# Another order of all queues for a routed attention with a gated dense block behind it

## The chip, the cores and the metric

The kernel runs on one core of one Trainium2 chip. A core has TensorE (PE, the matrix engine, whose weight loads are listed apart as PEld), VectorE (DVE), ScalarE (ACT), GpSimd (POOL), and SyncE (SP), which here only issues transfers. Each of them works through its own queue in the order in which the program was written; between the queues only semaphores order the work. The metric is the device time of one execution in microseconds; less is better.

## The reference

The inputs are q, k and v of 4 batches, 8 heads, 768 tokens and 64 values, and 16 centroids for each head. Every token of q and k is given to the centroid of its head that it is most alike, and a token of q attends only to the tokens of k with the same centroid:

```
mask   = q_assign[:, :, :, None] == k_assign[:, :, None, :]
scores = where(mask, q @ k.T / sqrt(D), -1e9)
attn   = softmax(scores);   a = attn @ v
x   = a, heads side by side          # 3072 x 512
h   = x @ w_in                       # 3072 x 1024
u   = h * softmax(h)
out = ((u - mean(u)) / sqrt(var(u) + 1e-6) * g_ln) @ w_out
```

## The kernel before

**The work.** A head's queries and keys are laid out with 64 rows of values and 16 or 32 rows of marks (which centroid), so that one product gives the score with the mask in it. The heads are taken in pairs, four pairs a batch, sixteen in all. For a pair, q and k are loaded by SyncE (`ld`), turned so that tokens lie along the free side (in batch 0 by TensorE, `tp`, and copied out of PSUM by `xa` and `xt`; later by VectorE, `xt`), cast to bf16 (`ca`), multiplied with the centroids (`cl` on TensorE), and the best centroid is found on VectorE (`tb`, `mx`, `oh`, `ot`) and placed as marks behind the cast values (`pl`; `bl` clears rows). v is loaded (`lv`) and cast (`cv`). Names carry batch, pair, q or k and half, so `ca0.2.1.1` is batch 0, pair 2, k, second half.

**The attention.** The scores are made in 144 regions of 1024 columns. `S` fills a region in two halves on TensorE (L641), `E` takes the exponential on ScalarE (L651), `V` multiplies with v on TensorE (six matmuls of 65 columns, L663), and `N` normalises on VectorE and frees the one bank that the V of a group write. Two PSUM regions are used in turn for S, so S of a region waits for the E two before. Batch 0 is regions 0 to 35.

**The dense block.** It runs on 24 tiles of 128 tokens, beside the attention of the next batch. x is turned by a transposing transfer (`tx`), `h` is the first product (four parts of two matmuls, L772), `hm` finds the maximum on VectorE and frees the bank, `ex` is the exponential on ScalarE, `u` the product with h, `tu` a transposing transfer, `bn`, `ag`, `as`, `al` the statistics, `y` the second product (L844) into one bank, `sc` scales it out of the bank, on ScalarE (L856) or VectorE (L858), and `ou` stores. The weights are loaded by `li` and `lo`, w_in is cast (`wi`), and w_out is centred by its column sums (`me`, `mf`, `ce`). The last tile is split finer and turned by TensorE (`ptx`, `ptu`).

**The order.** Nothing is planned when the kernel is built: each step is added under its name with the engine it may run on, and one list, `ORDER`, gives the sequence in which all 1568 steps are written. Each engine's queue is what falls to it from that list. A table, `AWAY`, names the steps that run on another engine than the one given in the code; `on(name, engine)` looks it up. The loop that writes the program is

```
for name in ORDER:
    o = self.ops[name]
    assert done.issuperset(o["first"]) and name not in done, name
    ...
    o["fn"]()
```

and it demands only that what a step needs has been written before it. A step that stands early in its engine's queue and waits holds everything behind it on that engine, transfers on SyncE included.

Of the kernel before, what the change touches and what calls it, by code (L numbers as in the profile page):

```python
# [45 lines left out]
E0 tp0.2.1.1 xt0.2.1 S1.0 tp0.3.0.0 S1.1 S2.0 S2.1 tp0.3.0.1 tb0.1 mx0.1 oh0.1 xa0.3.0 E1 E2 cl0.2  # L46
xt0.3.0 S3.0 S3.1 V0.0 V0.1 V1.0 S4.0 S4.1 V1.1 tp0.3.1.0 tb0.2 E3 S5.0 S5.1 E4 E5 ot0.1 N0 mx0.2
gt tp0.3.1.1 S6.0 S6.1 V2.0 V2.1 S7.0 S7.1 V3.0 V3.1 xa0.3.1 gk xt0.3.1 cl0.3 E6 E7 cv0.1.0
pl0.1.1.1 ca0.1.0.1 ca0.3.0.0 pl0.1.1.0 ca0.3.0.1 z2 ca0.1.1.1 oh0.2 pl0.1.0.0 pl0.1.0.1 gw S8.0
S8.1 S9.0 S9.1 me0 me1 ot0.2 tb0.3 pl0.2.1.0 N1 pl0.2.0.0 mx0.3 mk oh0.3 ca0.2.0.0 ca0.2.1.0  # L50
ca0.3.1.0 ca0.2.1.1 pl0.2.1.1 pl0.2.0.1 E8 E9 ca0.2.0.1 S10.0 S10.1 S11.0 S11.1 V4.0 V4.1 V5.0
V5.1 E10 S12.0 S12.1 cv0.2.1 E11 E12 mf N2 ot0.3 pl0.3.0.0 ld1.0.0.0 li0 ld1.0.0.1 ld1.0.0.2
ld1.0.0 ld1.0.1.0 lv0.3 ld1.0.1.1 ld1.0.1.2 ld1.0.1 cv0.1.1 ca0.3.1.1 pl0.3.1.0 pl0.3.0.1 cv0.2.0
cv0.3.0 cv0.3.1 wi0 S13.0 S13.1 V6.0 V6.1 S14.0 S14.1 V7.0 V7.1 pl0.3.1.1 N3 km ce0 E13 E14 S15.0
S15.1 S16.0 S16.1 E15 E16 V8.0 V8.1 S17.0 S17.1 E17 V9.0 V9.1 S18.0 S18.1 E18 S19.0 S19.1 N4 ce5
V10.0 V10.1 V11.0 V11.1 S20.0 S20.1 E19 S21.0 S21.1 E20 E21 li1 li3 N5 V12.0 V12.1 ptx0 S22.0
# [1298 lines left out]
```

## Time and profile before

| | |
|---|---|
| median of 3 runs | 222.33 us (221.85 to 222.96) |
| the profiled execution | 222.33 us |
| its span | 220.5 us |
| instructions | 6292 |
| granted TensorE clock | 1.00 in every stretch |

The profile's page gives first the busy time of each engine and its share of the span, then the span in forty slices, the chain of work that ended last, and groups of instructions by line. A row of the chain or of the order of time has the start in us, the length in us, the engine and line. A row of a group has the count, the busy time, the mean length in ns, and the idle time just before, with what ended it. A busy TensorE is not a TensorE at its peak, since its instructions overlap and may wait inside its pipe.

### The profile page before, as it was taken

The numbers are of one execution on the slowest core, as the hardware profiler recorded it, in microseconds if no ns is written. First come the engines' busy times: TensorE is split into PE (matmuls) and PEld (weight loads), VectorE is DVE, ScalarE is ACT, GpSimd is POOL, SyncE is SP. The second block draws the span as 40 slices with busy tenths as digits, with TensorE's granted clock in tenths as the row PEclk, the third lists the DMA queues.
The fourth block names the chain that finished last, engine by engine and source line by source line (L and its number), as shares of the span: only waits on it lengthen the run. The fifth ranks groups of instructions, "written<-read, shape, count | busy, mean of one in ns | idle before, by whom it ended". The sixth has DMA issues, their size and how long they took to land.

```text
span 220.5 us, 6292 instructions
## 1 busy us (share of the span) xinstructions
PE 211.4 (96%) x2401; PEld 148.9 (68%) x2431; DVE 185.7 (84%) x430; ACT 192.8 (87%) x245; POOL 158.8 (72%) x198
## 2 busy tenths in 40 slices
PE   7899999999999999999999999999999999999984
PEld 4567577677678776777677677666777767655442
DVE  3699979968999999896799999994888856989982
ACT  3799999999999998999999989999999888685362
POOL 3686969897898999549939997879889054456610
PEclk9999999999999999999999999999999999999999
DMA  5998999999999993999999981939584229777522
GB/s 199 394 402 259 189 175 300 126 154 259 164 154 169 190 188 62 174 248 210 153 225 162 180 184 38 171 92 209 151 173 90 72 64 168 154 120 170 163 94 100
DMA packets 120911, 38.33 MB, mean 174 GB/s; under 512 B 109993, under 2 KB 116401, under 8 KB 120881
## 3 DMA queue, kind: packets, MB, share of 16 engines
q1 hardware_dynamic: 120448, 37.40, 81.7%
q10 hardware_dynamic: 432, 0.52, 0.7%
q8 instruction: 19, 0.31, 0.6%
q14 instruction: 12, 0.09, 0.2%
HBM read 23.11 MB, written 6.29 MB: 133 GB/s over the span
## 4 chain that ended last, share of the span: by engine, by line
PE 72%; DVE 10%; DMA 6%; POOL 5%; issue 3%; ACT 2%; SPq 1%; DVEq 0%; ACTq 0%; POOLq 0%
PE sb L641 22%; PE hb L772 16%; PE mb L844 15%; PE ob L663 12%; DMA w_st<-in_moe_w_in_dram 4%; PE hb L470 3%; DMA raw<-in_q_dram 2%; DVE w_st L782 2%; PE hb L396 2%; DVE xt L421 2%; DVE bs L816 2%; POOL kbig L441 1%; PE mb L470 1%; POOL w_in_sb L580 1%; POOL v L556 1%
## 5 line engine op out<-in xcount | busy, mean ns | idle before, releaser
L651 ACT ACTIVATE e<-sb 128x1024 bf16<-128x1024 f32 x144 | 139.9, 1024 | 8.9 <-PE sb L641 8.1
L641 PE MATMUL sb<-qbig,kbig 80*128 80x256 bf16 (+3 forms) x648 | 83.8, 261 | 1.3 <-ACT e L651 1.0
L641 PEld LDWEIGHTS <-kbig 80*128 80x128 bf16 (+1 forms) x648 | 62.9, 119 | 25.4 <-issue 8.6
L805 POOL TENSOR_TENSOR u<-e_sb,w_st 128x1024 bf16<-128x1024 bf16 x21 | 45.1, 2145 | 20.0 <-ACT e_sb L798 13.3
L663 PEld LDWEIGHTS <-e 128*128 128x128 bf16 x1152 | 48.6, 97 | 10.4 <-DVE x L686 0.6
L663 PE MATMUL ob<-v,e 128*128 128x65 bf16 x1140 | 51.4, 193 | 0.2
L772 PE MATMUL hb<-w_in_sb,xT 128*128 128x512 bf16 x173 | 50.6, 379 | 0.9 <-POOL v L1323 0.3
L844 PE MATMUL mb<-w_out_c,uT 128*128 128x512 bf16 x165 | 45.5, 379 | 1.2 <-DVE y L858 0.4
L816 DVE BATCH_NORM_STATS2 bs<-u 128x6 f32<-128x512 bf16 x48 | 31.6, 680 | 1.1 <-POOL u L805 1.1
L798 ACT ACTIVATE e_sb<-w_st,nmax 128x1024 bf16<-128x1024 f32 (+1 forms) x25 | 27.8, 1113 | 3.2 <-DVE w_st L782 1.8
L439 POOL CAST qbig<-xt 64x768 bf16<-64x768 f32 (+1 forms) x31 | 25.7, 830 | 6.5 <-PE ob L663 2.7
L441 POOL TENSOR_SCALAR kbig<-xt 64x768 bf16<-64x768 f32 (+1 forms) x32 | 27.6, 865 | 2.4 <-DVE xt L409 0.8
L840 POOL TENSOR_TENSOR alpha<-var,halves 128x1 f32<-128x1 f32 x24 | 15.3, 638 | 12.6 <-DVE var L823 8.0
L421 DVE STREAM_TRANSPOSE xt<-raw 128x768 f32<-128x768 f32 x24 | 22.5, 959 | 0.1
L844 PEld LDWEIGHTS <-uT 128*128 128x128 bf16 x176 | 15.2, 97 | 10.2 <-issue 0.8
L772 PEld LDWEIGHTS <-xT 128*128 128x128 bf16 x192 | 15.8, 98 | 8.8 <-issue 0.6
L686 DVE TENSOR_TENSOR x<-ob,den 128x256 bf16<-128x256 f32 (+2 forms) x40 | 19.0, 474 | 1.4
L782 DVE TENSOR_SCALAR_CACHE_REDUCE w_st<-hb 128x512 f32<-128x512 f32 x24 | 16.3, 680 | 3.8 <-PE hb L772 3.7
L782 DVE TENSOR_SCALAR_CACHE_REDUCE w_st<-hb,nmax 128x512 f32<-128x512 f32 x24 | 17.8, 740 | 1.9 <-PE hb L772 1.5
L856 ACT ACTIVATE y<-mb,alpha 128x512 f32<-128x512 f32 x15 | 10.3, 685 | 6.5 <-POOL alpha L840 3.6
L675 DVE RECIPROCAL den<-ob 128x4 f32<-128x4 f32 (+2 forms) x40 | 7.1, 178 | 10.4 <-PE ob L663 10.1
L556 POOL CAST v<-vf 128x384 bf16<-128x384 f32 x22 | 10.9, 504 | 3.3 <-DMA vf<-in_v_dram 2.6
(109 smaller groups left out, 202.6 us busy)
## 6 DMA issues: line engine op xcount, KB each, us to landing
vf<-in_v_dram SPq DMA_DIRECT2D x16, 384.0 KB, 5.3
out_dram<-y SPq DMA_DIRECT2D x23, 256.0 KB, 2.5
raw<-in_k_dram SPq DMA_DIRECT2D x26, 192.0 KB, 4.6
raw<-in_q_dram SPq DMA_DIRECT2D x24, 192.0 KB, 5.1
...
raw<-in_q_dram SPq DMA_DIRECT2D x3, 384.0 KB, 6.6
raw<-in_k_dram SPq DMA_DIRECT2D x3, 384.0 KB, 7.6
```

The costliest lines, as they stand in the source:

```text
L421: nc.vector.transpose(xts[b, p, i][:], raw_of(b, p, i))
L439: (nc.vector if e == "DVE" else nc.gpsimd).tensor_copy(dst, src)
L441: (nc.vector if e == "DVE" else nc.gpsimd).tensor_scalar(dst, src, scalar1=inv_C, scalar2=1.0, op0=Alu.mult, op1=Alu.mult)
L641: nc.tensor.matmul(reg[:, c:c + wd], kb[u, pp, side_of(h), keys], qb[u, pp, side_of(h), su * P:su * P + wd])
L651: nc.scalar.activation(es[r][:, :w], src, Act.Exp, scale=exp_scale, bias=-exp_scale)
L663: nc.tensor.matmul(ops_of(group_of[n])[:, s, :VW], es[r][:, c0:c0 + P], v1[index[b, pair_of(h)] % R][:, side_of(h), kt, :VW], start=(kt == ...
L772: nc.tensor.matmul(hb[f2][:], xTs[f][:, dc, :], w_in_sb[:, dc, f2 * BANK:(f2 + 1) * BANK], start=(dc == 0), stop=(dc == n_dc - 1))
L782: nc.vector.tensor_scalar(ff[f, "h"][:, f2 * BANK:(f2 + 1) * BANK], hb[f2][:], scalar1=-1.0, scalar2=nmax[:, f2 - 1:f2] if f2 else 3.0e38, ...
L798: nc.scalar.activation(ff[f, "e"][:, cols(f, f2)], ff[f, "h"][:, cols(f, f2)], Act.Exp, bias=ff[f, "nmax"][:, n_ff2 - 1:], scale=-1.0, acc ...
L805: (nc.vector if e == "DVE" else nc.gpsimd).tensor_tensor(ff[f, "u"][:, cols(f, f2)], ff[f, "e"][:, cols(f, f2)], ff[f, "h"][:, cols(f, f2) ...
L816: nc.vector.bn_stats(ff[f, "bs"][:, f2, :], ff[f, "u"][:, f2 * BANK:(f2 + 1) * BANK])
L844: nc.tensor.matmul(y_of(f, x), ff[f, "uT"][:, fc, :], w_out_c[:, fc, parts_of(f, x)], start=(fc == 0), stop=(fc == n_fc - 1))
```

## The change

`AWAY` and `ORDER` are replaced. The set of the 1568 steps, their dependencies, the tiles and the buffers are the same; every queue has another order, and 77 steps run on another engine:

- from ScalarE to VectorE: the scalings sc6, sc7, sc8, sc11, sc17, sc22, the copy xa0.3.0 and the placing pl0.1.1.1; back: sc16 and xt0.2.1
- from ScalarE to GpSimd: four casts of q or k, eight of v, three placings; back: six casts of q or k, four of v, two placings
- from VectorE to GpSimd: nine `as`, eight placings, ce4 and ce5, bl1.2 and bl3.0, u20; back: five `as`, nine placings, bl2.0 and bl3.2, u0 and u15

On SyncE the first load of v stands behind three loads of tokens instead of one, the first load of w_in (`li0`) comes ahead of three of w_out's, and `lv0.3` ahead of batch 1's loads. The diff, cut to the table of engines, the start, the first steps of batch 1 and the end:

```diff
-    ca0.0.1.1.0 ca0.2.0.1 ca1.0.0.1 ca3.1.1.0 ca3.2.0.1 cv0.0.1 cv0.1.0 cv0.2.1 cv1.2.0
-    cv1.3.1 cv2.0.1 cv2.1.0 cv3.0.0 cv3.0.1 cv3.3.0 pl0.0.0.1 pl0.0.1.0 pl0.1.1.1 pl2.2.1.0
-    xa0.0.0 xa0.1.0 xa0.1.1 xa0.2.0 xa0.2.1 xa0.3.0 xt0.1.0 xt0.1.1 xt0.2.0 xt0.3.0
+    ca0.0.1.0.1 ca0.2.1.1 ca0.3.1.1 ca2.2.1.0 ca3.2.0.1 ca3.3.0.1 cv0.1.0 cv3.0.1 cv3.1.1
+    cv3.2.0 cv3.2.1 cv3.3.1 pl0.0.0.0 pl0.0.1.1 xa0.0.0 xa0.1.0 xa0.1.1 xa0.2.0 xa0.2.1
+    xt0.1.0 xt0.1.1 xt0.2.0 xt0.2.1 xt0.3.0
...
-    as0 as11 as14 as15 as17 as18 as19 as2 as22 as23 as4 as5 as9 bl1.2 bl3.0 ce0 ce2 ce4 km mk
...
-    pl1.2.0.0 pl2.0.0.0 pl2.0.0.1 pl2.0.1.1 pl2.2.0.0 pl3.0.0.1 pl3.2.0.1 pl3.2.1.0 sc0 sc1
-    sc12 sc13 sc14 sc16 sc4 sc9
+    as1 as12 as13 as14 as17 as18 as2 as20 as8 bl2.0 bl3.2 ce0 ce2 km mk pl0.0.1.0.0 pl0.1.1.1
+    pl0.2.1.0 pl0.2.1.1 pl0.3.0.1 pl0.3.1.0 pl0.3.1.1 pl1.0.0.0 pl1.0.1.0 pl1.0.1.1 pl1.2.0.0
+    pl1.2.1.0 pl2.0.0.0 pl2.0.1.0 pl2.0.1.1 pl2.2.0.0 pl3.0.1.1 pl3.2.0.0 pl3.2.1.0 sc0 sc1
+    sc11 sc12 sc13 sc14 sc17 sc22 sc4 sc6 sc7 sc8 sc9
...
-lc ld0.0.0.0 ld0.0.1.0 ld0.0.0 ld0.0.1 ld0.1.0 ld0.1.1 lv0.0 ld0.2.0 ld0.2.1 ld0.3.0 lo3 lv0.1
-ld0.3.1 lg lv0.2 lo1 lo2 lo0 cx z5 cy cz wu tp0.0.0.0 tp0.0.0.1 tp0.0.1.0 tp0.0.1.1 cp xa0.0.0
-xt0.0.0 xa0.0.1 xt0.0.1 tp0.1.0.0 xa0.1.0 cb cl0.0 tb0.0 mx0.0 oh0.0 ot0.0 ca0.0.0.0.0 z3
-ca0.0.1.0.0 ca0.0.0.0.1 cc ca0.0.0.1.1 ca0.0.0.1.0 pl0.0.1.1 pl0.0.0.0 ca0.0.1.0.1 ca0.0.1.1.1
-ca0.0.1.1.0 tp0.1.0.1 tp0.1.1.0 xt0.1.0 xa0.1.1 cl0.0.1 tp0.1.1.1 cv0.0.1 xt0.1.1 pl0.0.0.1
-tp0.2.0.0 tp0.2.0.1 tb0.0.1 mx0.0.1 oh0.0.1 ot0.0.1 pl0.0.1.0.1 pl0.0.1.0.0 pl0.0.1.1.1 cl0.1 sg
-pl0.0.1.1.0 z1 ca0.1.1.0 cv0.0.0 ca0.1.0.0 xa0.2.0 pl0.0.1.0 tp0.2.1.0 xt0.2.0 xa0.2.1 S0.0 S0.1
+lc ld0.0.0.0 ld0.0.1.0 ld0.0.0 ld0.0.1 ld0.1.0 ld0.1.1 lg ld0.2.0 ld0.2.1 ld0.3.0 lv0.0 lo0
+ld0.3.1 li0 lo2 lo3 lo1 lv0.1 lv0.2 cx cy cz wu tp0.0.0.0 tp0.0.0.1 tp0.0.1.0 tp0.0.1.1 xa0.0.0
+xt0.0.0 ca0.0.0.0.1 xa0.0.1 cp tp0.1.0.0 cb cl0.0 tb0.0 mx0.0 oh0.0 ot0.0 xt0.0.1 ca0.0.1.0.1
+xa0.1.0 tp0.1.0.1 xt0.1.0 tp0.1.1.0 xa0.1.1 tp0.1.1.1 xt0.1.1 cl0.0.1 tp0.2.0.0 tp0.2.0.1 tb0.0.1
+mx0.0.1 oh0.0.1 ot0.0.1 pl0.0.1.0.0 cl0.1 tb0.1 pl0.0.1.0.1 ca0.0.0.0.0 ca0.0.0.1.0 ca0.0.1.0.0
+ca0.0.0.1.1 cc ca0.0.1.1.0 ca0.1.0.0 pl0.0.1.0 pl0.0.0.1 sg ca0.0.1.1.1 pl0.0.1.1.1 pl0.0.1.1.0
+pl0.0.1.1 pl0.0.0.0 xa0.2.0 tp0.2.1.0 xt0.2.0 xa0.2.1 S0.0 S0.1 E0 tp0.2.1.1 tp0.3.0.0 S1.0 S1.1
...
-S28.1 E28 V16.0 V16.1 V17.0 S29.0 S29.1 h0.1.0 V17.1 S30.0 S30.1 E29 E30 oh1.0 hm0.0 N8 ot1.0 ce2
-pl1.0.1.0 pl1.0.0.1 pl1.0.1.1 bl1.0 ce3 lv1.0 tx2 lv1.1 lv1.2 ld2.0.0.0 ld2.0.0.1 ld2.0.0.2 h0.1.1
-S31.0 S31.1 V18.0 V18.1 V19.0 S32.0 S32.1 V19.1 h1.0.0 N9 hm0.1 pl1.0.0.0 xt1.2.0 E31 S33.0 S33.1
+S28.1 E27 E28 V16.0 V16.1 V17.0 S29.0 S29.1 V17.1 h0.0.1 S30.0 S30.1 oh1.0 N8 h0.1.0 E29 E30 S31.0
+S31.1 E31 V18.0 V18.1 V19.0 S32.0 S32.1 V19.1 h0.1.1 ot1.0 pl1.0.1.1 hm0.0 pl1.0.1.0 N9 pl1.0.0.0
+xt1.2.0 hm0.1 S33.0 S33.1 h1.0.0 ca1.0.0.1 ca1.0.0.0 pl1.0.0.1 ca1.0.1.0 ca1.1.0.1 z4 ca1.0.1.1
...
-y20.0 y20.1 y20.2 y20.3 sc20 hm23.0 bn22.0 h23.1.1 ptu22.0 ptu22.1 bn22.1 hm23.1 tu22.1 tu22.0
-ex23.0 ex23.1 ou19 y21.0 y21.1 y21.2 y21.3 ou20 u23.0 u23.1 ag22 as23 ptu23.0 ptu23.1 tu23.1
-bn23.0 bn23.1 ag23 al21 sc21 ou21 tu23.0 y22.0 y22.1 y22.2 y22.3 y23.1.0 y23.1.1 y23.1.2 y23.1.3
-y23.0.0 y23.0.1 y23.0.2 y23.0.3 al22 sc22 al23 sc23.0 sc23.1 ou23.1 ou22 ou23.0
+y20.2 y20.3 sc20 h23.1.1 hm23.0 hm23.1 ptu22.0 ptu22.1 bn22.0 tu22.1 ex23.0 ex23.1 tu22.0 y21.0
+y21.1 y21.2 y21.3 ou19 ou20 as22 al21 as23 u23.0 u23.1 bn22.1 bn23.0 ag22 ptu23.0 ptu23.1 sc21
+ou21 tu23.0 y22.0 y22.1 y22.2 y22.3 tu23.1 bn23.1 ag23 al22 al23 y23.1.0 y23.1.1 y23.1.2 y23.1.3
+y23.0.0 sc22 y23.0.1 y23.0.2 y23.0.3 sc23.0 sc23.1 ou23.1 ou22 ou23.0
```

More of the change, by code (lines that the diff above doesn't have):

```diff
@@ L45 @@
-pl0.0.1.1.0 z1 ca0.1.1.0 cv0.0.0 ca0.1.0.0 xa0.2.0 pl0.0.1.0 tp0.2.1.0 xt0.2.0 xa0.2.1 S0.0 S0.1
[L46 to L56, printed above, removed]
@@ new lines @@
+ca0.0.0.1.1 cc ca0.0.1.1.0 ca0.1.0.0 pl0.0.1.0 pl0.0.0.1 sg ca0.0.1.1.1 pl0.0.1.1.1 pl0.0.1.1.0
+pl0.0.1.1 pl0.0.0.0 xa0.2.0 tp0.2.1.0 xt0.2.0 xa0.2.1 S0.0 S0.1 E0 tp0.2.1.1 tp0.3.0.0 S1.0 S1.1
+S2.0 S2.1 xt0.2.1 cl0.2 E1 E2 S3.0 S3.1 E3 mx0.1 xa0.3.0 oh0.1 ot0.1 cv0.0.0 ca0.1.0.1 cv0.0.1
+ca0.1.1.0 tp0.3.0.1 V0.0 V0.1 V1.0 S4.0 S4.1 V1.1 S5.0 S5.1 tp0.3.1.0 xt0.3.0 pl0.1.0.0 pl0.1.1.0
+pl0.1.0.1 ca0.2.1.0 ca0.1.1.1 tb0.2 pl0.1.1.1 mx0.2 N0 xa0.3.1 tp0.3.1.1 gt gk xt0.3.1 E4 E5 S6.0
+S6.1 E6 V2.0 V2.1 S7.0 S7.1 E7 ca0.2.1.1 V3.0 cl0.3 S8.0 S8.1 S9.0 S9.1 V3.1 ca0.3.1.0 gw oh0.2
@@ new lines @@
+ot0.2 tb0.3 pl0.2.1.0 mx0.3 oh0.3 N1 ot0.3 me0 E8 S10.0 S10.1 E9 E10 pl0.2.0.0 ca0.3.0.0 z1
+ca0.2.0.0 ca0.2.0.1 pl0.2.0.1 ca0.3.0.1 ca0.3.1.1 cv0.1.0 cv0.1.1 pl0.3.0.0 me1 S11.0 S11.1 V4.0
+V4.1 V5.0 S12.0 S12.1 V5.1 mk E11 E12 pl0.2.1.1 N2 mf lv0.3 z2 cv0.2.1 cv0.2.0 z3 cv0.3.0 cv0.3.1
+ld1.0.0.0 ld1.0.0.1 ld1.0.0.2 ld1.0.0 ld1.0.1.0 ld1.0.1.1 ld1.0.1.2 ld1.0.1 pl0.3.0.1 pl0.3.1.1
+pl0.3.1.0 km li2 li1 wi0 li3 ce1 ce5 ce6 wi1 wi2 wi3 S13.0 S13.1 V6.0 V6.1 S14.0 S14.1 V7.0 V7.1
+N3 E13 S15.0 S15.1 E14 S16.0 S16.1 E15 V8.0 V8.1 V9.0 S17.0 S17.1 V9.1 E16 E17 S18.0 S18.1 ce0 N4
```

162 lines of the change are left out of this document (81 added, 81 removed).

## The prediction

> **What bounds the kernel now.** I read the busy shares first, then the busy time by stretches, then the chain of waits over the first 60 us, and last the order of time on ScalarE and at the end. The stretches are cut where the first scores start (12.24 us), where batch 0 has handed over to batch 1 (50.89) and at the last product (217.35); the columns are busy us (count) of PE, weight loads, DVE, ACT, POOL, then clock, DMA share, GB/s.
>
> ```profile
> span 220.5 us, 6292 instructions
> ...
> PE 211.4 (96%) x2401; PEld 148.9 (68%) x2431; DVE 185.7 (84%) x430; ACT 192.8 (87%) x245; POOL 158.8 (72%) x198
> ```
> ```profile
> 0.00:12.24 12.24, 10.31 (x65) 5.86 (x65) 6.31 (x25) 7.08 (x15) 6.37 (x25) 1.00 0.84 307
> ...
> 12.24:50.89 38.65, 37.17 (x496) 27.07 (x497) 33.66 (x69) 37.77 (x45) 32.21 (x45) 1.00 1.00 220
> 50.89:217.35 166.46, 163.93 (x1844) 116.01 (x1870) 145.28 (x337) 147.95 (x187) 120.25 (x130) 1.00 0.80 154
> ```
>
> The profiled execution took 222.33 us, 1.8 over its span, and is the median of the runs shown, so a change of the span carries over one to one. TensorE is busy throughout, but busy includes waiting in its pipe, so I count its work by the shortest lengths in which its pieces follow each other in the chain of waits:
>
> ```profile
> 12.95 0.33 PE hb L396 x3
> ...
> 16.31 0.55 PE ob L663 x18
> 16.86 0.44 PE sb L641 x4
> 17.30 0.18 PE ob L663 x6
> ...
> 50.84 0.43 PE hb L772 x2
> ...
> 53.76 0.78 PE hb L470 x8
> ```
>
> A region of scores (S) is 0.44, a product with v (V, six matmuls) 0.18, a part of the first dense layer (h) 0.43, a part of the second (y) I take like h, a turn of tokens (tp) 0.33, a clustering (cl) 0.78. From S0 to S36, which is the stretch 12.24 to 50.89, the old order puts 36 regions, 44 V, 7 h, 5 tp and 4 cl on TensorE: 15.8 + 7.9 + 3.0 + 1.7 + 3.1 = 31.5, and the column sums of w_out and four small steps add some 3. That is 34.5 of 38.65. ScalarE in the same stretch:
>
> ```profile
> 12.99 1.02 ACT L651 ACTIVATE e<-sb 128x1024 bf16<-128x1024 f32 x1
> 13.95 0.48 ACT L407 COPY xt<-hb 128x384 f32<-128x384 f32 x1
> ...
> 21.95 0.51 ACT L529 COPY kbig<-oht 32x384 f32<-32x384 f32 x1
> ...
> 24.44 0.84 ACT L437 ACTIVATE qbig<-xt 64x768 bf16<-64x768 f32 x1
> ...
> 26.22 0.51 ACT L554 CAST v<-vf 128x384 bf16<-128x384 f32 x1
> 26.63 12.27 ACT L651 ACTIVATE e<-sb 128x1024 bf16<-128x1024 f32 x13
> ...
> 41.06 0.84 ACT L437 ACTIVATE qbig<-xt 64x768 bf16<-64x768 f32 x1
> ```
>
> It is busy 37.77 of 38.65, and thirteen exponentials (E) follow each other at 0.94 without a gap. So ScalarE sets the pace to 50.89 and TensorE has some 4 us spare there. After that it turns round: the count from S36 to the last product (108 regions 47.5, 148 V 26.6, 89 h 38.3, 99 y of which eight are half length 40.8, 10 cl and the last turns 8.5) is some 162 of 166.46. TensorE sets the pace there, and only its order of waits could be improved.
>
> **The change, part by part.** Nothing is added or removed; 1568 steps stand in another order and 77 of them change their engine. ScalarE has 9 fewer steps, VectorE 2 more, GpSimd 7 more.
>
> *The start.* The first load of v goes behind three loads of tokens on SyncE's queue, the tiny load of g ahead of them.
>
> ```profile
> GB/s 199 394 402 259 189 175 300 126 154 259 164 154 169 190 188 62 174 248 210 153 225 162 180 184 38 171 92 209 151 173 90 72 64 168 154 120 170 163 94 100
> ...
> vf<-in_v_dram SPq DMA_DIRECT2D x16, 384.0 KB, 5.3
> ```
> ```profile
> 8.88 0.86 ACT L407 COPY xt<-hb 128x384 f32<-128x384 f32 x2
> ...
> 9.62 0.64 DVE L505 STREAM_TRANSPOSE oht<-oh 128x192 bf16<-128x192 bf16 x2
> 9.76 0.51 ACT L554 CAST v<-vf 128x384 bf16<-128x384 f32 x1
> ...
> 10.34 0.20 PEld L396 LDWEIGHTS hb<-ident_f,raw 128*128 128x128 f32 x2 [0.47 <-ACT v L554]
> ```
> ```profile
> 11.25 0.78 PE mb L470 x8
> 12.03 0.48 PE hb L396 x3
> 12.51 0.44 PE sb L641 x4
> ```
>
> At the 394 GB/s of the second slice a load of 384 KB takes 1.0 us, so the tokens of pair 2 land that much sooner, and the cast of v (0.51, at 9.76) leaves ScalarE's queue for GpSimd's, where V0 needs it only after 16 us. The turn at 10.34 then starts at about 9.95, the clustering of pair 1 (cl0.1, at 11.25) waits for its bank until 10.65 and ends at 11.4. The placings of the first marks wait for the turn that ends at 9.62 + 0.64 = 10.26 as before; two of them (0.35 each) now run on ScalarE ahead of the copy xa0.2.0, which so starts at 11.05 as before, and the turn behind it on TensorE at 11.6 instead of 12.03. S0 and E0 come 0.4 earlier. Bounds: 0.9 (turn and loads both early) and +0.3 (a cast of pair 1 now stands ahead of two placings on GpSimd and can hold them).
>
> *ScalarE from E0 to E35.* It loses xa0.3.0 (0.48), pl0.1.1.1 and cv0.2.1 (0.51 each), ca0.2.0.1 and ca1.0.0.1 (0.84 each), 3.18 together, and takes xt0.2.1 (0.48), ca0.2.1.1 and ca0.3.1.1 (0.84 each), 2.16. Net 1.0 less, on the engine that sets the pace. What leaves it lands on GpSimd and VectorE, the casts mostly on GpSimd.
>
> ```profile
> L439 POOL CAST qbig<-xt 64x768 bf16<-64x768 f32 x27 | 23.7, 879 | 5.0 <-PE ob L663 2.7 <-PE sb L641 1.1 <-ACT xt L407 0.4
> ...
> L556 POOL CAST v<-vf 128x384 bf16<-128x384 f32 x22 | 10.9, 504 | 3.3 <-DMA vf<-in_v_dram 2.6
> ```
>
> At 0.88 and 0.50 these are hidden as long as pair 2 is ready for S12 and pair 3 for S15, which I followed along GpSimd's new queue: from the widening of g at about 20.8 on, the last cast of pair 2 ends near 24.7 (S12 is due at 25.5), that of pair 3 near 26.1 and its last placing, on VectorE, near 28.3 (S15 due 28.9). Without that cover each would cost what it is late. The casts of w_in then end near 39.5, ahead of the first h at about 40.4. Three late placings of pair 1.0 are on VectorE before S36 instead of one.
>
> ```profile
> 45.48 0.18 DVE L675 RECIPROCAL den<-ob 128x4 f32<-128x4 f32 x1 [1.25 <-PE ob L663]
> ...
> 46.93 0.71 DVE L618 SCALAR_TENSOR_TENSOR w_out_c<-w_g,g_ln,y 128x512 bf16<-128x512 f32 x1
> ...
> 49.30 1.16 DVE L531 COPY qbig<-oht 32x768 f32<-32x768 f32 x1
> ```
> ```profile
> L531 DVE COPY qbig<-oht 32x768 f32<-32x768 f32 x7 | 4.9, 702 | 0.2
> ```
>
> They add 1.4 (two at 0.70) to 2.3 (two at 1.16), the centring at 46.93 (0.71) has left that place, and one h part more (0.43) stands on TensorE in between; so S36 is 0.3 to 1.2 worse than level there, of which the old order has 0.4 spare (50.46 to 50.89). I take 0 and keep 0.8 for the range.
>
> *TensorE from S36.* One h part of seven has moved behind S36, out of the stretch where it cost nothing: +0.4.
>
> *The last stretch.* Two statistics steps of tile 22 no longer stand ahead of the last maximum.
>
> ```profile
> 209.14 1.28 DVE L816 BATCH_NORM_STATS2 bs<-u 128x6 f32<-128x512 bf16 x2
> ...
> 209.71 0.38 PE L772 MATMUL hb<-w_in_sb,xT 128*128 128x512 bf16 x1
> ...
> 210.34 0.73 DVE L782 TENSOR_SCALAR_CACHE_REDUCE w_st<-hb,nmax 128x512 f32<-128x512 f32 x1
> 210.63 0.58 ACT L768 COPY w_g<-sb 128x512 bf16<-128x512 bf16 x1
> ```
>
> It can start at about 210.0 instead of 210.34. Against that the copy at 210.63 goes behind the two last exponentials, and the scaling of tile 22 moves to VectorE ahead of the last one. Taken together -0.3, between -0.8 and +0.5.
>
> *All the rest* (orders between 51 and 209 us, SyncE's queue included): the counts above bound the gain by the 4 us that the stretch has over its work; I take 0, since the distances in TensorE work between a step and what it waits for are alike in the two orders: least distance from a region to the V that needs its exponential 1.59 before and 1.41 after, from a scaled y to the next tile's first y 0.50 in both.
>
> Sum: -0.4 - 1.0 + 0.4 - 0.3 = -1.3, so 222.33 - 1.3 = 221.0 us.
>
> **The rivals.** *More comes out.* Besides its work ScalarE waited about 1 us in the stretch to 50.89, and TensorE has some 4 us beyond its count after it. If the new order also clears 1.5 of these 5, it ends at 219.5. For it: nothing but the slack; against: the distances are alike. Chance 0.12.
>
> ```profile
> L858 DVE TENSOR_SCALAR y<-mb,alpha 128x512 f32<-128x512 f32 x8 | 5.9, 736 | 1.8 <-POOL alpha L840 1.2 <-PE mb L844 0.7
> ...
> L856 ACT ACTIVATE y<-mb,alpha 128x512 f32<-128x512 f32 x15 | 10.3, 685 | 6.5 <-POOL alpha L840 3.6 <-PE mb L844 2.9
> ```
>
> *ScalarE sets the pace after 50.89 too.* Its 147.95 of 166.46 there, the most after TensorE, speaks for it, and TensorE's weight loads fill only 116.01. The five scalings net that leave it (0.69 each by the second row) then give 3.4 more: 217.6. The h at 0.43 and S at 0.44 back to back and their count of 162 speak against it. Chance 0.04. The Trainium skill, page "Perfetto Trace Analysis", section "Identifying the Most-Contended Engine", is on this rival's side: TensorE's headroom is to be read from the share of its weight loads (68% here), not from that of its matmuls.
>
> *It is given back.* ScalarE runs ahead, and TensorE, which has the same work, arrives at 51 us no sooner: the waits move to S36 and the first V of batch 1 behind GpSimd, where casts of q and k, two of v and a centring of w_out now stand behind one placing that waits for a turn on VectorE. 222.3. For it: TensorE is busy 37.17 of 38.65 in that stretch; against: only 34.5 of that is work. Chance 0.15.
>
> *VectorE becomes the bound: slower.* Six scalings (sc6, 7, 8, 11, 17, 22) move to VectorE and one away, one product u more net.
>
> ```profile
> DVE den L675 <- PE ob L663: 10.1, 17, 1.3
> ```
>
> Five net at 0.736 are 3.7, the rest of the moves about 0.4 more: VectorE would be busy 190 of 220. Everything that frees TensorE's banks (normalising, maxima, turns) waits behind them. Now normalising waits for TensorE (10.1 us), not the reverse, which speaks against; 145.28 of 166.46 in the long stretch speaks for it. If three quarters of the 4.1 reach TensorE the time is 221.0 + 3.1 = 224.1; above 2.4 it is slower by more than the bound below. Chance 0.24. The Trainium skill (page "SBUF — State Buffer", section "Who interferes with whom") says that VectorE's copies in a two-port mode and GpSimd shut each other out for a whole instruction. The copy of 1.16 against the mean of 702 ns fits it; by that rule the three late placings more that VectorE takes would cost up to 0.46 each on top, 1.4, and the sum would be 222.4, a case that ends like the rival before.
>
> **How the numbers follow.** Forecast 0.45 (its own range 220.2 to 221.9), rivals 0.12, 0.04, 0.15, 0.24. About 0.5% or 1.1 us is what a measurement of this kernel can tell from no change. Faster than 221.2: two thirds of the forecast (0.30) and the first two rivals, with 0.46 rounded to 0.45. Same: the rest of the forecast and most of the third rival, 0.28. Slower: what is left, mostly the fourth rival, 0.27. The range 219.4 to 224.0 leaves out the second rival, half of the fourth and a little of the first.
>
> **What would show it.** Right: the first exponential at about 12.5; ScalarE's busy time from E0 to E35 down by 1.0; S36 at about 49.5; the long stretch no more than 0.5 longer; the last maximum directly behind the last h. Wrong: TensorE waiting at S36 or at the first V of batch 1 for GpSimd, V or h waiting for VectorE between 94 and 190 us, or exponentials in the first stretch with gaps released by GpSimd's or VectorE's placings.

## The result, and the profile after

The changed kernel takes 223.88 us (median; 223.47 to 224.08) where the kernel before takes 222.33 (221.85 to 222.96): ratio 1.007, 95% interval 1.0045 to 1.0094. It is slower by 1.5 us, and two later measurements of the same pair say the same: 223.64 against 222.21 (1.0060, 1.0033 to 1.0086) and 223.48 against 222.00 (1.0074, 1.0047 to 1.0101).

The page of the changed kernel (the last row is the chain of waits by engine), and its busy time by stretches, cut at its own first scores, first scores of batch 1 (S36) and last product (columns as in the prediction):

```profile
span 222.3 us, 6278 instructions
...
PE 211.5 (95%) x2397; PEld 148.5 (67%) x2431; DVE 191.3 (86%) x431; ACT 187.1 (84%) x236; POOL 160.6 (72%) x208
...
PE 76%; DVE 12%; ACT 4%; issue 3%; DMA 2%; SPq 1%; DVEq 0%; ACTq 0%
```
```profile
0.00:12.21 12.21, 10.05 (x65) 5.78 (x65) 6.09 (x24) 7.32 (x15) 7.13 (x24) 1.00 0.85 295
12.21:49.99 37.78, 36.51 (x494) 26.70 (x495) 33.84 (x69) 36.23 (x42) 32.54 (x45) 1.00 0.96 236
49.99:218.05 168.06, 164.90 (x1841) 116.03 (x1872) 150.84 (x339) 143.32 (x180) 120.96 (x140) 1.00 0.77 150
218.05:222.30 4.25, 0.00 (x0) 0.00 (x0) 0.48 (x1) 0.27 (x1) 0.00 (x0) 0.80 0.36 125
```

The start is as long as before (12.21 against 12.24). The stretch in which ScalarE sets the pace is 0.87 shorter, ScalarE's busy time in it 1.5 less. The long stretch, in which TensorE sets the pace, is 1.6 longer, and what follows it 1.1. (The clock of 0.80 stands in a stretch without a product; a pair of traces below has 1.00 there and shows the same longer end.)

Since one h part has moved across the second cut, and a busy TensorE may be waiting, I kept an account in another way: for every step of TensorE the time since the first scores, less the shortest lengths of all steps in between. That sum can only rise by waiting, and a rise has a place. I call it the account. The last column but one runs from the start of the last product to the end. In us:

```
trace                         waits of TensorE from            last product  span
                              S0     S36    h12.0.0   all      to the end
                              to S36 to h12 to last
before                        4.30   2.57   1.87      8.74     3.54          220.5
changed                       3.86   2.87   2.74      9.47     4.59          222.3
changed, second trace         3.86   2.89   2.73      9.49     4.65          222.5
changed, third trace          3.23   2.91   2.75      8.90     4.56          222.3
```

(h12.0.0 is at about 142 us. The first scores themselves come between 11.95 and 12.90 us in most traces of either order and at 14.0 to 14.4 in three, with the landing of the first loads; the account leaves that out.) In the first pair: -0.44 at the front, +0.30 and +0.87 behind it, +1.05 at the end, together +1.78, the difference of the spans.

Where the account jumps in the changed kernel behind S36 and did not before, TensorE waits for VectorE. The order of time at the three places (start, length, engine and line, and in brackets the idle time and what ended it):

```profile
72.85 0.34 PE L663 MATMUL ob<-v,e 128*128 128x65 bf16 x6 [0.52 <-DVE x L686]
```
```profile
120.39 0.37 PEld L470 LDWEIGHTS hb<-xt,c_bd 128*32 128x32 f32 x4 [0.26 <-DVE xt L421]
121.25 0.14 PEld L470 LDWEIGHTS hb<-xt,c_bd 128*32 128x32 f32 x4 [0.49 <-DVE xt L421]
```
```profile
153.63 1.24 PE L844 MATMUL mb<-w_out_c,uT 128*128 128x512 bf16 x5 [0.27 <-DVE y L858]
```

The first is V33 waiting for normalisation N14 (+0.58 in the account), the second the clustering cl3.1 waiting for the transposes xt3.1 (+0.74, where other traces have +0.19), the third the product of tile 9 waiting for the scaling sc8 (+0.33, and +0.32 in two small waits around it, at 149.8 and 158.4). VectorE ahead of each:

```profile
70.20 0.92 DVE L531 COPY kbig<-oht 32x768 f32<-32x768 f32 x1
71.15 0.98 DVE L421 STREAM_TRANSPOSE xt<-raw 128x768 f32<-128x768 f32 x1
72.05 0.16 DVE L675 RECIPROCAL den<-ob 128x6 f32<-128x6 f32 x1
72.24 0.56 DVE L686 TENSOR_TENSOR x<-ob,den 128x384 bf16<-128x384 f32 x1
...
119.36 1.83 DVE L421 STREAM_TRANSPOSE xt<-raw 128x768 f32<-128x768 f32 x2
...
145.72 3.40 DVE L493 TENSOR_TENSOR oh<-cst,mx 128x768 bf16<-128x768 f32 x1
...
152.83 0.75 DVE L858 TENSOR_SCALAR y<-mb,alpha 128x512 f32<-128x512 f32 x1
```

N14 stands behind a placing and a transpose that nobody needs yet. The comparison oh3.2 at 145.72 takes 3.40 us and makes all that follows late, sc8 at 152.83 among it. In the kernel before it took 0.95:

```profile
147.39 0.95 DVE L493 TENSOR_TENSOR oh<-cst,mx 128x768 bf16<-128x768 f32 x1
```

The account also shows what the front owes to a load. In the kernel before, an h part waits at 43 us for the last piece of w_in:

```profile
41.72 1.04 POOL L580 CAST w_in_sb<-w_st 128x1024 bf16<-128x1024 f32 x1 [0.80 <-DMA w_st<-in_moe_w_in_dram]
```
```profile
42.81 0.38 PE L772 MATMUL hb<-w_in_sb,xT 128*128 128x512 bf16 x1 [0.33 <-POOL v L1323]
```

(The releaser named is a short step directly behind that cast.) It costs 0.49 here and 1.04 and 0.34 in two more traces of the old front; no trace of the new front has it. There `li0` is loaded ahead of three of w_out's pieces and the casts of w_in end earlier, counted from the first scores. Whether it is `li0` that does it was not tried alone.

### The profile page after: what moved, and what is told of

It reads as the page before. It is cut to its first block, busy times and chain, and to the rows that moved or that the text cites. A ratio compares the mean times of both kernels' runs of the same rounds, so it can differ in the third digit from the quotient of the medians.

```text
span 222.3 us, 6278 instructions
## 1 busy us (share of the span) xinstructions
PE 211.5 (95%) x2397; PEld 148.5 (67%) x2431; DVE 191.3 (86%) x431; ACT 187.1 (84%) x236; POOL 160.6 (72%) x208
## 4 chain that ended last, share of the span: by engine, by line
PE 76%; DVE 12%; ACT 4%; issue 3%; DMA 2%; SPq 1%; DVEq 0%; ACTq 0%
PE sb L641 24%; PE mb L844 15%; PE hb L772 15%; PE ob L663 13%; PE hb L470 4%; DMA raw<-in_q_dram 2%; ACT e L651 2%; DVE w_st L782 2%; PE hb L396 2%; DVE bs L816 2%; PE mb L470 1%; DVE xt L421 1%; DVE w_out_c L618 1%; DVE x L686 1%; DVE y L858 1%
## 5 line engine op out<-in xcount | busy, mean ns | idle before, releaser
L641 PE MATMUL sb<-qbig,kbig 80*128 80x256 bf16 (+3 forms) x648 | 81.6, 261 | 0.9 <-ACT e L651 0.5
L805 POOL TENSOR_TENSOR u<-e_sb,w_st 128x1024 bf16<-128x1024 bf16 x20 | 43.0, 2153 | 14.3 <-issue 7.0
L772 PE MATMUL hb<-w_in_sb,xT 128*128 128x512 bf16 x173 | 49.6, 379 | 0.6
L844 PE MATMUL mb<-w_out_c,uT 128*128 128x512 bf16 x162 | 46.0, 378 | 1.3 <-DVE y L858 0.3
L441 POOL TENSOR_SCALAR kbig<-xt 64x768 bf16<-64x768 f32 (+1 forms) x30 | 25.8, 861 | 4.0 <-DVE den L675 2.4
L844 PEld LDWEIGHTS <-uT 128*128 128x128 bf16 x176 | 14.7, 97 | 11.3 <-issue 1.1
L840 POOL TENSOR_TENSOR alpha<-var,halves 128x1 f32<-128x1 f32 x24 | 13.7, 573 | 9.7 <-DVE var L823 7.2
L556 POOL CAST v<-vf 128x384 bf16<-128x384 f32 x26 | 13.9, 542 | 0.8
L835 POOL TENSOR_SCALAR es<-esum 128x1 f32<-128x1 f32 x14 | 3.4, 246 | 14.2 <-ACT e_sb L798 13.2
L856 ACT ACTIVATE y<-mb,alpha 128x512 f32<-128x512 f32 x10 | 6.9, 688 | 7.7 <-PE mb L844 5.1
```

Source lines behind the costliest of these rows:

```text
L441: (nc.vector if e == "DVE" else nc.gpsimd).tensor_scalar(dst, src, scalar1=inv_C, scalar2=1.0, op0=Alu.mult, op1=Alu.mult)
L641: nc.tensor.matmul(reg[:, c:c + wd], kb[u, pp, side_of(h), keys], qb[u, pp, side_of(h), su * P:su * P + wd])
L772: nc.tensor.matmul(hb[f2][:], xTs[f][:, dc, :], w_in_sb[:, dc, f2 * BANK:(f2 + 1) * BANK], start=(dc == 0), stop=(dc == n_dc - 1))
L805: (nc.vector if e == "DVE" else nc.gpsimd).tensor_tensor(ff[f, "u"][:, cols(f, f2)], ff[f, "e"][:, cols(f, f2)], ff[f, "h"][:, cols(f, f2) ...
L844: nc.tensor.matmul(y_of(f, x), ff[f, "uT"][:, fc, :], w_out_c[:, fc, parts_of(f, x)], start=(fc == 0), stop=(fc == n_fc - 1))
```

## The experiments

Each kernel was measured beside the kernel before on one chip; "trace" is its own profiled execution. In the variants line numbers are two lower. Edits are shown as the order within one engine's queue.

**The tail.** The scaling of tile 22 goes back to ScalarE in the changed kernel, and to VectorE in the kernel before:

```diff
-    sc11 sc12 sc13 sc14 sc17 sc22 sc4 sc6 sc7 sc8 sc9
+    sc11 sc12 sc13 sc14 sc17 sc4 sc6 sc7 sc8 sc9
```

Expected of the first, and of the second:

> The changed kernel with one edit: the scaling of tile 22 goes back from VectorE to ScalarE. Theory A (the tail): from the last product of the output to the end of the program the changed kernel takes 4.8 us against 3.75 us before, because this scaling stands on VectorE behind the statistics of tile 23 and runs at 217.21 instead of 215.72, so that the store of tile 22 is issued with the last ones. Then the scaling runs at about 216.0 to 216.4, its store is issued before 217.5, and the time falls by 0.6 to 1.1 us against the changed kernel, to 222.8 to 223.3. Rival B (the end is set by the last maximum and by the stores of tile 23 alone, wherever tile 22 is scaled): within 0.2 us of the changed kernel, 223.7 to 224.1.

> The kernel before with the same edit alone: the scaling of tile 22 goes to VectorE, behind the statistics of tile 23. Theory A (the tail): it runs at about 216.5 to 216.8 instead of 215.72, its store is issued close to those of tile 23, and the time rises by 0.5 to 1.0 us, to 222.8 to 223.4. Rival B: no change, 222.1 to 222.5. If only the second of the pair moves the time, the tail depends on what else stands behind the scaling.

Measured: 223.80 us (223.00 to 224.19; 1.0075, 1.0055 to 1.0096), and 222.35 against 222.15 (1.0012, 0.9998 to 1.0026). The first trace had the tail down to 3.59 us, with waits unchanged at 9.47, but the median had not moved; the second had a tail of 3.56, as without the edit. Both medians spoke for the rival, the first trace against it. So I ran the first of them once more beside the changed kernel, and a second pair that differs in the same one step, made of the mended variant told below:

> The changed kernel, unaltered, beside the next one. Theory A (the tail is part of the loss): 223.5 to 223.9 us, 3.4 us or more from the issue of the last store to the end. Rival B (an accident of the traces): the same time, and in this trace 2.4 us.

> The changed kernel with the scaling of tile 22 on ScalarE, once more. Theory A: 0.7 to 1.1 us under the changed kernel beside it, 222.5 to 223.0 us; the first median (223.80) came from executions that began late (their trace had the first product of scores 0.6 us later). Rival B: within 0.3 us of the changed kernel beside it.

> The changed kernel with four repairs (N14 ahead of one transpose, bn6.1 and bn7.0 behind N24, u11 behind one cast, the scaling of tile 22 on ScalarE), once more: 220.6 to 221.2 us, faster than the kernel before.

> The same with three repairs: the scaling of tile 22 stays on VectorE, as in the changed kernel. Theory A: 0.7 to 1.1 us over the one with four, 221.6 to 222.1 us, and three stores issued within 0.8 us at the end. Rival B: within 0.3 us of the one with four.

Measured in the same order: 223.48, 222.82, 220.88 and 221.43 us (against 222.00; intervals of the ratios 1.0047 to 1.0101, 1.0015 to 1.0065, 0.9924 to 0.9971, 0.9956 to 0.9988). With the scaling on VectorE the median is 0.66 higher in one pair and 0.55 in the other, a little under what theory A said and more than the rival's 0.3. But in both pairs the two intervals overlap, and the first run of the same edit had given nothing; so the price in time is known only roughly. What makes the difference shows in the traces of the mended pair; first with the scaling on VectorE, then on ScalarE (a row of SPq with x2 covers two stores, from the first issue to the end of the second):

```profile
214.62 0.75 DVE L856 TENSOR_SCALAR y<-mb,alpha 128x512 f32<-128x512 f32 x1
```
```profile
215.40 1.08 SPq L866 DMA_DIRECT2D out_dram<-y  x2
```
```profile
213.80 0.69 ACT L854 ACTIVATE y<-mb,alpha 128x512 f32<-128x512 f32 x1 [1.64 <-POOL alpha L838]
215.23 0.47 ACT L854 ACTIVATE y<-sb,alpha 128x256 f32<-128x256 f32 x1 [0.74 <-POOL alpha L838]
215.73 0.35 ACTq L866 DMA_DIRECT2D out_dram<-y  x1
```
```profile
214.52 1.90 SPq L866 DMA_DIRECT2D out_dram<-y  x2
```

The last product starts at 215.1 in both. With the scaling on VectorE the 256 KB of tile 22 are issued at 215.40 and the last 128 KB 0.74 later; on ScalarE 0.88 earlier, 1.56 ahead of the last. From the issue of the last store to the end it is 3.46 against 2.62 us, with a granted clock of 1.00 in both. Over all traces: 3.46 to 3.62 in six of seven where the three last stores are issued within 0.71 to 0.76 us (the seventh 2.91), 2.5 to 2.9 where they are spread over 1.16 us or more. The kernel before with the scaling on VectorE had them over 1.16 us (217.68, 218.20, 218.84), which fits its losing nothing: in these traces the end is longer when the three stores come together, not by the engine as such.

**The front.** All queues in the new order and on the new engines up to S36, from there on those of the kernel before:

> Every queue in the changed kernel's order and on its engines up to the products S36 of scores and all that it issues before them, and from there on the order and the engines of the kernel before for all that is left. Theory A (the front is a gain that the later stretches take back): TensorE has waited 0.5 to 0.7 us less than before by 50 us, as in the changed kernel, and the rest costs what it costs in the kernel before: 221.6 to 221.9. Rival B (what the front saves is owed to work that it puts off, and comes due wherever the rest is done): 222.2 to 222.6, with the difference gone by 80 us.

Measured: 222.84 us against 222.15 (1.004, 1.0021 to 1.0059), slower. The waits to S36 were 3.87, as in the changed kernel, but 3.52 behind, in place of 2.57. The jump is one:

```profile
55.76 0.52 PE L661 MATMUL ob<-v,e 128*128 128x65 bf16 x12 [0.92 <-POOL v L554]
```
```profile
53.52 1.28 POOL L622 TENSOR_TENSOR w_out_c<-w_g,y 128x512 bf16<-128x512 f32 x1
54.75 1.41 POOL L554 CAST v<-vf 128x384 bf16<-128x384 f32 x2
```

The first V of batch 1 waits for casts of v that stand behind a centring of w_out. The next variant exchanges them on GpSimd:

```diff
 z5 ca1.1.0.0 ca1.1.1.0 bl1.0
-ce3 cv1.0.0 cv1.0.1
+cv1.0.0 cv1.0.1 ce3
```

> The front of the changed kernel and the rest of the kernel before, as run already, with two casts of v (cv1.0) ahead of one piece of the output weights (ce3) on GpSimd. There TensorE had waited 0.4 us less than in the kernel before by 48 us, counted from the first product of scores, and 0.98 us at 55.9 for the first of these casts. Theory A (the wait at 55.9 is a seam between two orders and no debt of the front): it goes, nothing comes in its place, and the time is 221.6 to 222.0 us. Rival B (GpSimd is behind by then, and the work put off falls due there or a little later): another wait of 0.4 us or more between 56 and 75 us, 222.3 to 222.9 us.

Measured: 221.17 us (220.87 to 221.81; 0.9951, 0.9931 to 0.9970), faster than the kernel before. The waits behind S36 are 2.44, no wait took the place of the one at 55.9, and those to S36 are 3.23. So the front of the change is a real gain, and the wait came from joining two orders. But the gain, 0.4 to 1.1 us in the account, is no more than what one misplaced cast takes away.

**Four repairs of the changed kernel.** On VectorE (and the scaling of tile 22 on ScalarE):

```diff
 hm4.0 pl1.2.0.0 as1 pl1.2.1.0
-xt2.0.0 N14 hm4.1
+N14 xt2.0.0 hm4.1
...
-sc4 bn6.1 hm8.1 pl2.2.0.0 N23 xt3.0.1 hm9.0 bn7.0 hm9.1 xt3.1.0 xt3.1.1 N24
+sc4 hm8.1 pl2.2.0.0 N23 xt3.0.1 hm9.0 hm9.1 xt3.1.0 xt3.1.1 N24 bn6.1 bn7.0
...
-oh3.2 hm13.0 bn9.1 hm13.1 ag9 ot3.2 hm14.0 sc8 bn10.0
+hm13.0 bn9.1 bn10.0 hm13.1 oh3.2 ag9 ot3.2 hm14.0 sc8
```

> The changed kernel with four edits: the scaling of tile 22 back on ScalarE; the normalisation N14 ahead of one transpose of tokens; the statistics bn6.1 and bn7.0 behind normalisation N24, so that the transposes xt3.1 come 1.3 us earlier; the comparison oh3.2, which took 3.40 us beside an elementwise product on GpSimd, behind the maximum hm13.1. Theory A (single waits on VectorE and the tail make the loss, and each can be taken away by itself): 0.6 to 1.1 us of the tail, 0.5 us at 72 us, 0.6 us at 121 us and 0.3 us at 153 us go, and the time falls to 221.5 to 222.1, at or under the kernel before. Rival B (VectorE is short of time as a whole, 86% busy, so a wait taken away at one place comes back at the next): 223.0 to 223.6, the gain of the tail alone.

Measured: 223.67 us (1.0082, 1.005 to 1.0114), not under 222.1 as theory A had it. The first two repairs did all they should: waits from S36 to h12 fell from 2.87 to 1.60, with no jump at 73 us and 0.19 at 121. The third was wrong. oh3.2 took 2.98 us at its new place too, and tile 9 now waited 1.99 for sc8. What the two places have in common stands on GpSimd. In the changed kernel, GpSimd beside oh3.2:

```profile
144.58 1.62 POOL L441 TENSOR_SCALAR kbig<-xt 64x768 bf16<-64x768 f32 x2
146.17 2.14 POOL L805 TENSOR_TENSOR u<-e_sb,w_st 128x1024 bf16<-128x1024 bf16 x1
148.28 1.54 POOL L441 TENSOR_SCALAR kbig<-xt 64x768 bf16<-64x768 f32 x1
```

The comparison (two inputs in on-chip memory) is over at 149.1, 0.8 after the product u11 is, and the cast behind u11 takes 1.54 instead of 0.8. In the four-repairs variant the product beside it is u12, at 149.03. The next variant leaves VectorE's order as the change has it and exchanges two steps on GpSimd; it ran beside the changed kernel itself:

```diff
 ca3.3.1.0 ca3.2.1.0
-u11.0 ca3.1.1.0 al8
+ca3.1.1.0 u11.0 al8
```

> The changed kernel once more, unaltered, as the measure for the variants beside it. What its first trace showed at one place each: (1) from the issue of the last store to the end 3.4 us, where the kernel before and four variants had 2.4; (2) the first product of scores at 12.21 us, where variants with the same first 12 us had 11.95 to 12.90. Theory A: the 1.0 us behind the last store belongs to the change (the store of tile 22 is issued 0.74 us ahead of the last one instead of 1.6) and is there again. Rival B: it was an accident of one execution, and is not there again; then the tail is worth no more than 0.1 us. Time by either: 223.3 to 224.2 us.

> The changed kernel with two steps of GpSimd exchanged: the elementwise product u11 (two inputs, 2.14 us) goes behind one cast of keys. Theory A (a comparison of VectorE with two inputs in on-chip memory stands still while GpSimd does an elementwise product with two inputs there): the comparison oh3.2, which took 3.40 us beside u11 at 145.7 and 2.98 us beside u12 when it was put behind the maximum hm13.1, is over before u11 starts and takes 0.95 us; the products of tile 9 of the output no longer wait for the scaling of tile 8, and TensorE waits 0.3 to 0.5 us less by 156 us. Rival B (the length has to do with what oh3.2 reads or writes): 3 us again, and the wait of 0.33 us with it.

Measured: 223.64 and 222.56 us (222.33 to 224.69; 1.0016, 0.9992 to 1.0041), 1.1 us less by that exchange. The unaltered kernel again has its long end (3.62 us from the last issue). In the variant's trace, VectorE and then GpSimd:

```profile
145.26 2.12 DVE L491 TENSOR_TENSOR oh<-cst,mx 128x768 bf16<-128x768 f32 x1
```
```profile
144.12 2.42 POOL L439 TENSOR_SCALAR kbig<-xt 64x768 bf16<-64x768 f32 x3
146.51 2.88 POOL L803 TENSOR_TENSOR u<-e_sb,w_st 128x1024 bf16<-128x1024 bf16 x1
```

oh3.2 waits for the casts (they too read on-chip memory), runs at 146.5, and this time u11 is the one held: 2.88 instead of 2.14. The 0.95 that I expected was wrong; but the 1.3 us saved are enough, the wait for sc8 is gone, with sc8 still on VectorE, and waits from h12 on are 1.98 instead of 2.73. In the account of the two traces 0.75 of the 1.37 us is this; 0.63 is the tie told below. With the two good repairs of VectorE's order, this exchange and the scaling of tile 22 on ScalarE together:

> The changed kernel with u11 behind one cast of keys on GpSimd, the normalisation N14 ahead of one transpose of tokens, the statistics bn6.1 and bn7.0 behind normalisation N24, and the scaling of tile 22 back on ScalarE. In the variant with four repairs the waits at 73 us (0.58) and 121 us (0.55 of 0.74) were gone, and the comparison that it moved made a new one of 1.99 us at 154.8. Theory A (the loss of the changed kernel is these single waits, the collision among them): TensorE's waits behind the first product of scores sum to 0.6 to 1.0 us less than in the kernel before by 210 us, and the time is 221.2 to 221.9 us, faster than the kernel before. Rival B (waits come back elsewhere as VectorE is short): 222.5 to 223.3 us.

Measured: 220.83 us (220.12 to 221.02) against 222.21 (0.9924, 0.9894 to 0.9953), and 220.88 when it ran again: faster than both kernels, by 1.1 to 1.4 and by 2.6 to 2.8 us. That is under the 221.2 to 221.9 of theory A. Its waits sum to 6.84, against 8.74 before and 9.47 in the changed kernel, or 8.90 in the trace of it that has the tie told below in its favour. The pieces add up: 0.75 (account) to 1.1 (medians) for the exchange on GpSimd, 0.55 to 0.66 for the scaling, and 1.27 of waits for the two orders on VectorE make 2.6 to 3.0, where 2.8 was measured side by side. The trace of the second run, page and chain of waits:

```profile
span 218.7 us, 6276 instructions
...
PE 87%; ACT 6%; DMA 2%; issue 2%; SPq 1%; DVE 0%; DVEq 0%; ACTq 0%
```
```profile
49.37:215.45 166.08, 163.75 (x1841) 115.81 (x1872) 148.94 (x338) 144.09 (x181) 121.27 (x140) 1.00 0.79 152
```

VectorE has left the chain, of which it had 12% in the changed kernel and 10% in the kernel before, though it is still busy for 148.94 of 166.08 there.

**The collision, in the kernel before.** There u11 runs at 150.0, after the comparison. The comparison, at 147.39, comes 0.02 ahead of a cast on GpSimd, and it is the cast that is held: three casts of 0.8 take 3.39 us.

```profile
146.52 3.39 POOL L441 TENSOR_SCALAR kbig<-xt 64x768 bf16<-64x768 f32 x3
```

With u11 moved ahead:

```diff
 al9
-ca3.3.1.1 ca3.3.1.0 ca3.2.1.1 u11.0
+u11.0 ca3.3.1.1 ca3.3.1.0 ca3.2.1.1
```

> The kernel before with one step of GpSimd moved: the elementwise product u11 goes ahead of three casts of keys, to about 146.5 us, so that it runs where VectorE starts the comparison oh3.2 (147.4 us, 0.95 us long). Theory A (of a two-input operation on VectorE and one on GpSimd, both out of on-chip memory, the second stands still until the first is done): oh3.2 takes 2.0 to 2.4 us, or, if it starts first, u11 takes 0.9 us longer than its 2.14. TensorE's products are little held, time within 0.3 us of the kernel before. Rival B (the comparison was long in the changed kernel for another reason): 0.95 us for oh3.2 and 2.14 us for u11.

Measured: 222.29 us against 222.11 (1.0009, 0.9987 to 1.003), no difference in time. VectorE and GpSimd in its trace:

```profile
149.35 1.97 DVE L491 TENSOR_TENSOR oh<-cst,mx 128x768 bf16<-128x768 f32 x1
```
```profile
148.36 2.14 POOL L803 TENSOR_TENSOR u<-e_sb,w_st 128x1024 bf16<-128x1024 bf16 x1
```

As theory A has it, if just under its 2.0 to 2.4: 1.97 instead of 0.95, until 0.8 us after u11's end. TensorE has no step behind it that is short of time there, and so nothing is lost.

**The tie.** A second pair of that kind came with the change: ce5 moved from VectorE to GpSimd, and its two-input step now starts where VectorE starts ce2. In the changed kernel's trace VectorE's ce2 and GpSimd's step, and then the two in the variant with u11 later:

```profile
32.25 1.85 DVE L618 SCALAR_TENSOR_TENSOR w_out_c<-w_g,g_ln,y 128x512 bf16<-128x512 f32 x1
```
```profile
32.29 1.27 POOL L624 TENSOR_TENSOR w_out_c<-w_g,y 128x512 bf16<-128x512 f32 x1
```
```profile
32.38 0.74 DVE L616 SCALAR_TENSOR_TENSOR w_out_c<-w_g,g_ln,y 128x512 bf16<-128x512 f32 x1
```
```profile
32.43 1.83 POOL L622 TENSOR_TENSOR w_out_c<-w_g,y 128x512 bf16<-128x512 f32 x1
```

With starts 0.04 apart either engine may be the one that waits. Where it is VectorE, a normalisation behind it is late and the products V12, with the turn of x behind them, wait 0.62 at 35.6: that is the 3.86 against 3.23 in the account. It came out the one way in six traces with this front and the other way in seven, and two kernels have shown both. I moved ce2 to where VectorE is idle:

```diff
-N3 ce0 N4 ce2 xt1.0.0
+N3 ce0 ce2 N4 xt1.0.0
```

> The changed kernel with one step of VectorE moved: the piece ce2 of the output weights (two inputs, 0.74 us) goes ahead of normalisation N4, into 1.06 us in which VectorE waits. In the changed kernel ce2 starts at 32.25 us, 0.04 us ahead of the two-input step of ce5 on GpSimd; in five traces of that front it took 1.85 us and the transposes of x waited 0.62 us at 35.8, in three it took 0.74 us, GpSimd's step took 1.83 instead of 1.26 us, and nothing waited. Theory A (a tie for the same access, won by either): ce2 takes 0.74 us, the wait at 35.8 is gone in every run, 0.3 to 0.6 us less than the changed kernel in the median, 223.0 to 223.4. Rival B (the wait has another cause): it is there in the trace, 223.6 to 223.9.

> The changed kernel with five repairs: ce2 ahead of normalisation N4; N14 ahead of one transpose of tokens; bn6.1 and bn7.0 behind N24; u11 behind one cast of keys; the scaling of tile 22 back on ScalarE. Against the variant with four of them (220.83 us) the tie at 32.3 us can no longer be lost. Theory A (the repairs are independent of each other): 220.2 to 220.9 us, and waits behind the first product of scores 1.3 to 1.7 us under the kernel before. Rival B (with ce2 early, N4 and the products V10 behind it come later, or something else takes the place): 220.9 to 221.5.

Measured: 223.68 us (1.0061, 1.0038 to 1.0083) and 221.13 us (220.12 to 222.40; 0.9947, 0.9925 to 0.9969). The wait at 35.8 was gone in both traces, but nothing was gained in the median. ce2 now collides with a cast of w_in (1.52 us), V10 waits 0.51 for N4 instead of 0.30, and the waits to S36 are 3.40, between the two outcomes of the tie. That the tie costs executions without a profile as often as those with one was not shown.

**VectorE's load.** Five of the six scalings back on ScalarE, sc8 ahead of E115:

```diff
-    sc11 sc12 sc13 sc14 sc17 sc22 sc4 sc6 sc7 sc8 sc9
+    sc12 sc13 sc14 sc22 sc4 sc9
```

> The changed kernel with the scalings of tiles 6, 7, 8, 11 and 17 back on ScalarE (the one of tile 8 ahead of exponential E115); the scaling of tile 22 stays on VectorE. Rival A (VectorE is loaded to the bound by the scalings moved to it, the fourth rival of the prediction): with five of 0.74 us gone from it, the waits of TensorE behind the first product of scores sum to 0.8 us or more less than in the changed kernel, and the time is 222.2 to 222.8. Theory B (two collisions of two-input operations, two queue orders and the tail make the loss, wherever the scalings run): only the wait of the products of tile 9 (0.33 us at 153.8) can go, the waits at 73 us (0.59) and 122 us (0.75) stay as they are, ahead of the first of the five, and the time is 223.2 to 223.7.

Measured: 226.10 us (225.53 to 227.51; 1.0178, 1.0149 to 1.0207), slower than either theory had it. The waits at 73 and 122 us stayed at 0.59 and 0.74, as B said; but new ones came, TensorE and then ScalarE in the trace:

```profile
138.20 1.02 PE L842 MATMUL mb<-w_out_c,uT 128*128 128x512 bf16 x4 [0.77 <-ACT y L854]
...
173.09 0.59 PE L842 MATMUL mb<-w_out_c,uT 128*128 128x512 bf16 x2 [1.17 <-ACT y L854]
```
```profile
136.54 1.02 ACT L649 ACTIVATE e<-sb 128x1024 bf16<-128x1024 f32 x1 [0.42 <-PE sb L639]
137.46 0.68 ACT L854 ACTIVATE y<-mb,alpha 128x512 f32<-128x512 f32 x1
```

A scaling that stands behind an exponential waits until TensorE has made that exponential's scores, and TensorE's next tile waits for the scaling. So in this order the moves to VectorE relieve TensorE. The edit changes place along with engine, so it doesn't price VectorE's load alone. The mended variant says more on that: it is the fastest of all, with five of the six scalings on VectorE.

## Why the prediction was wrong

221.0 us was forecast, 1.3 less than before, and 223.88 came, 1.5 more. It lies inside the range, on the side of the fourth rival, but the main line of the prediction failed, in two terms of its sum. "All the rest", put at 0 because distances in TensorE's work are alike in the two orders, cost 1.2 us of waits for VectorE. "The last stretch", put at -0.3, came to +1.0 in the traces, since nothing had been said of the store behind the moved scaling. Step by step:

- **The start, -0.4: nothing.** The cast of v left ScalarE's queue and the turn at 10.34 did not move:

```profile
9.40 0.55 PE L396 MATMUL hb<-ident_f,raw 128*128 128x128 f32 x3 [0.24 <-ACT xt L407]
...
9.88 0.53 PE L470 MATMUL mb<-xt,g_wide 128*32 128x192 f32 x8
...
10.34 0.64 PEld L396 LDWEIGHTS hb<-ident_f,raw 128*128 128x128 f32 x6 [0.30 <-issue]
```

  The clustering cl0.0.1 (0.53) used to stand ahead of the turn at 9.56 and now stands behind it, ahead of the turn in question, which so starts at 10.34 again. I had followed ScalarE's queue and the loads past the new order, not TensorE's own. From the turn at 7.3 to the first scores it is 4.86 to 4.88 us in most traces of the new order and 4.89 in two of the old one.
- **ScalarE to E35, -1.0: right in mechanism.** From the first exponential to the end of the 36th ScalarE is busy 38.04 before and 36.67 after, 1.4 less instead of 1.0. The time itself is 38.79 before and 37.92 after (37.29 where the tie goes well). That it comes out near -1.0 is partly luck: the tie at 32 us takes 0.63 of it or not, and the old front's wait for w_in is worth 0.3 to 1.0 to TensorE (the prediction had put SyncE's queue at nothing). With the longest and the shortest of these waits the kernel before had 39.83 and 38.63 in two more traces. The account gives TensorE 0.44 to 1.07 of the gain.
- **One h part behind S36, +0.4: as costed**, S36 at 49.99 instead of the expected 49.5 for want of the start.
- **The last stretch, -0.3, between -0.8 and +0.5: failed, +1.0.** The last maximum does stand directly behind the last h (at 210.90, when TensorE ended its wait of 0.38), but from that h to the last product only 0.1 is gained (7.52 us before, 7.44 after). "The scaling of tile 22 moves to VectorE ahead of the last one" was costed at its place among the engines; the store behind it was not followed. Its issue moved from 1.57 to 0.74 us ahead of the last store, and three stores that come together end 0.8 to 1.0 later in most traces. In the medians the scaling on VectorE is 0.55 to 0.66 slower, with intervals that overlap.
- **All the rest, 0: failed, +1.2.** I had compared distances in TensorE's work, which say nothing of what stands ahead of a step in VectorE's queue. +0.30 to h12.0.0 is N14 (0.58) and cl3.1 (0.55 over 0.19), less waits of the old order that are gone; of the +0.87 behind it, 0.75 is the collision and what it makes late. The count of TensorE's work that bounded this term has one slip, 99 parts of y for 100; with it the sum is still some 162.
- **The fourth rival: right in sign, wrong in mechanism.** That its 224.1 is near the 223.88 is luck. TensorE did wait for VectorE, though not quite at the products named: a V at 73 us, a clustering at 121 and a y at 154. But two of the three places go when three steps change their place in VectorE's queue, and the third when two steps change on GpSimd, with VectorE busy for 148.94 us of the long stretch instead of 150.84. Of the Trainium skill's page "SBUF — State Buffer", section "Who interferes with whom", I had used the rule on copies and passed over the one that decides here: that a VectorE instruction with two inputs in SBUF contends with a GpSimd instruction that reads SBUF. The 3.40, 2.98 and 1.97 us for a comparison of 0.95 agree with it. The prediction's own use of that section, 1.4 us for three late placings, was not tested.
- **The third rival** names the first V of batch 1 behind GpSimd: not in the changed kernel, but its front with the old rest met just this, 0.98 us at 55.9.
- **The first two rivals are out.** No more came out than was counted on. In the long stretch ScalarE had 4.6 us less to do (143.32 against 147.95) and the stretch became 1.6 longer, so ScalarE does not set the pace there. In the mended kernel the chain is 87% TensorE's and 6% ScalarE's. The Trainium skill's page "Perfetto Trace Analysis", section "Identifying the Most-Contended Engine", would read TensorE's headroom from its share of the peak arithmetic rate or from that of its weight loads, 68% in the kernel before; the chain and the account of 6.8 us of waits say otherwise.
